# Mixing product ahead of phi of q in the queue of small work of 23 attention steps, and the second halves of the first two h scaled by Pool

## The chip, the cores and the metric

One core of a Trainium2 chip. The metric is the device time of one execution in microseconds (us). All runs but two are in the fast state, with a granted TensorE clock of 1.0: one run of the kernel before took 736.96 us and is left out of every comparison, and the single look of pool_probe (clock 0.996) is of unknown state and is compared with nothing. "TensorE" is the matrix engine (PE, with PEld for its weight loads), "VectorE" is DVE, "ScalarE" is ACT, "Pool" is GpSimd.

## The reference

It adds three things: the input x, a causal linear-memory attention over its layer norm, and a token-mixing MLP over the layer norm of that norm. Sizes: 2048 tokens, 1024 channels, 32 heads of 32, four segments of 512 tokens, 3584 hidden units.

```python
def _A_ref(x, wq, wk, wv, wo, beta):
    # q, k, v = x @ wq, x @ wk, x @ wv, as (B, H, N=4 segments, L=512, Dh=32)
    phi = lambda t: jnp.where(t > 0, t + 1.0, jnp.exp(t))
    for s in range(N):
        p = _softmax(jnp.einsum('bhqd,bhkd->bhqk', qs, ks) * scale + mask)
        a_dot = jnp.einsum('bhqk,bhkd->bhqd', p, vs)
        pq = phi(qs)
        a_mem = jnp.einsum('bhld,bhde->bhle', pq, M) / (jnp.einsum('bhld,bhd->bhl', pq, z)[..., None] + 1e-06)
        outs.append(g * a_mem + (1.0 - g) * a_dot)
        M, z = M + (phi(ks) against vs), z + (sum of phi(ks))
    return o @ wo

def _B_ref(x, w1, b1, w2, b2):
    h = _layernorm(x)
    u = _gelu(jnp.einsum('bsd,sf->bdf', h, w1) + b1)
    return transpose(jnp.einsum('bdf,fs->bds', u, w2) + b2)

x = A_x; xn = _layernorm(x)
return x + _A_ref(xn, ...) + _B_ref(xn, ...)
```

## The kernel before

The MLP runs first (until about 385 us), then the attention, in 32 steps: step u computes unit u (one segment, four heads) and finishes unit u-1. In the traces VectorE's operations of a step stand in the order in which they are issued (step 15 before: mtmp 515.49, pqT 515.81, prod 516.42). Semaphores are set from the lists `reads` and `writes`.

**The head.** The first rows are normalised while TensorE already waits for them. In the order string, `S` is the reciprocal root (a small addition on VectorE, then a power on Pool), `h` the scaling of a row, and a `'` marks its second half of 512 columns:

```python
NORM_ORDER = (["D0 A1 A1' A3 S0 h0 h0' S1 d2 h1 d2' S2 h1' h2 d4 A3' A5 S3 d4' h3"] + ...)

def rstd(self, c):                                   # "S"
    fw.op("dve", ... var = var * a + E_H)            # L609
    fw.op("pool", ... rs = pow(var, expo))           # L611

def scale_h(self, c, parts):                         # "h", "h'"; rows 0 and 1 in two halves
    for h0, h1 in parts:
        self.fw.op("dve", lambda e: e.tensor_scalar(both[:, h0:h1, c // 2, :], src, self.ln_mv[:, c, 0:1],
                                                    self.ln_rs[:, c, 1:2], op0=ALU.subtract, op1=ALU.mult), ...)  # L627
```

**The attention.** VectorE makes phi of q in two operations (`mtmp`, `pqT`), and the mixing of a unit's two outputs in four (`srec` twice, the mixing product `prod`, the sum `o_s`). Pool masks the exponentials of ScalarE. One group of matmuls, `weigh`, reads `pqT`:

```python
def phi(self, dst, R_dst, src, R_src, k, u):
    fw.op("dve", ... tensor_scalar(mt, et, 1.0, None, op0=ALU.min))                              # L1241, mtmp
    fw.op("dve", ... scalar_tensor_tensor(dst, src, 1.0, mt, op0=ALU.add, op1=ALU.max))          # L1243, pqT

def logits(self, u, step): ...
    fw.op("act", ... pT = exp(scores))                                                           # L1377
    for v, kb, _ in blocks:
        fw.op("pool", lambda e: e.affine_select(d, d, ...))                                      # L1381, the mask

def weigh(self, u, part): ...
    reads += [self.R_pqT[k], self.R_MZbf[g]]      # beside pT and vA: the group starts when all are there

def combine(self, u): ...
    return [scales, products, add]                # srec (L1474, L1475), prod (L1478), o_s (L1484)

def wo_job(self, c, half): ...
    def end(b): fw.op("dve", ... fin = bank + fin)          # L1320: also hands the bank back to TensorE

# the step u
    self.dense(cuts[0]); self.logits(u, 0); self.dense(cuts[1], end)
    self.weigh(u - 1, 0) ... self.weigh(u - 1, 2)            # with pieces of dense work between
    steps = self.combine(u - 1)
    self.side.append(steps.pop(0))                           # srec
    if N_GRP <= u:
        self.side.append(lambda u=u: self.phi_q(u))          # mtmp, pqT
    self.side.extend(steps)                                  # prod, o_s
    self.side.append(lambda u=u: (self.phi_k(u + 1), self.k_transpose(u + 1)))
    ...                                                      # dense, logits(u, 1); even steps also logits(u, 2)
```

`self.side` is a queue of small work that is issued, piece by piece, between the matmuls. `pqT` of unit u is thus made in step u and read by `weigh(u, 0)` in step u+1.

## Time and profile before

| | before |
|---|---|
| median (fast runs) | 652.8 us |
| span of the profiled run | 651.1 us |
| TensorE busy | 645.8 us |
| VectorE, ScalarE, Pool busy | 428.1, 281.4, 153.9 us |

Busy time says that TensorE is full, but not how full (the prediction says why). What matters is a hole between two starts. A line of a timeline reads: start, length (us), engine, source line, operation, output<-inputs, shape, how many instructions in a row; in brackets the idle time of the engine before it and what ended that. The lines themselves are in the prediction.

### The profile page before, as it was taken

Reading aid. Unit: us, or ns where it says so; the run is one execution under the profiler, and the core shown is the slowest. Engines: PE = TensorE matmul, PEld = TensorE weight load, DVE = VectorE, ACT = ScalarE, POOL = GpSimd, SP = SyncE. Lnnn points to the kernel's source line nnn. Section 1 sums busy time; section 2 is a strip of 40 time slices with the busy share of each in tenths; the row PEclk is TensorE's granted clock in tenths of the full one; section 3 lists DMA queues with packets and bytes.
Section 4 is the critical chain, followed back from the end, with each engine's and each line's share of the span. In section 5 each row is a group of like instructions: output and inputs, shape, how many; then the busy total and the mean of one; then the engine's idle time right before and its main releaser. Section 6 shows DMA issues by size and latency. Waiting matters only on the chain.

```text
span 651.1 us, 11170 instructions
## 1 busy us (share of the span) xinstructions
PE 645.8 (99%) x4611; PEld 303.2 (47%) x4611; DVE 428.1 (66%) x800; ACT 281.4 (43%) x305; POOL 153.9 (24%) x179
## 2 busy tenths in 40 slices
PE   8999999999999999999999999999999999999998
PEld 3444444444444444444444444444544444445544
DVE  6975675665556664744738325766787877777896
ACT  7543232232210000110101047778767778888770
POOL 2500000000011220220202203343334444554440
DMA  9804233242498967538262946988544456445325
GB/s 306 212 0 130 65 106 89 64 116 79 129 257 206 270 205 209 156 103 229 80 208 98 267 126 174 179 169 197 120 116 96 125 147 109 126 98 128 106 93 139
DMA packets 181963, 95.00 MB, mean 146 GB/s; under 512 B 100248, under 2 KB 167832, under 8 KB 181656
## 3 DMA queue, kind: packets, MB, share of 16 engines
q1 hardware_dynamic: 181768, 94.25, 56.3%
q8 instruction: 36, 0.59, 0.4%
q14 instruction: 15, 0.12, 0.1%
q10 hardware_dynamic: 144, 0.03, 0.0%
HBM read 69.23 MB, written 13.63 MB: 127 GB/s over the span
## 4 chain that ended last, share of the span: by engine, by line
PE 91%; DVE 5%; ACT 2%; DMA 2%; issue 1%; POOL 0%; DVEq 0%
PE ps_all L199 91%; ACT pT L1377 1%; DMA w2s<-in_B_w_dram 1%; DVE prod L1478 1%; DVE ln_st L587 1%; DVE sum L648 0%; DMA xin<-in_A_x_dram 0%; DVE mtmp L1243 0%; DVE h L627 0%; DVE mtmp L1241 0%; DVE fin L1320 0%; DVE ost L1431 0%; DVE kT L1275 0%; POOL ln_rs L611 0%; DVE part L689 0%
## 5 line engine op out<-in xcount | busy, mean ns | idle before, releaser
L1377 ACT ACTIVATE pT<-ps_all 128x2048 bf16<-128x2048 f32 x80 | 150.2, 1877 | 47.7 <-PE ps_all L199 47.2
L1381 POOL TENSOR_SCALAR_AFFINE_SELECT pT<-pT 128x512 bf16<-128x512 bf16 x128 | 105.3, 841 | 161.3 <-ACT pT L1377 161.3
L689 DVE TENSOR_TENSOR part<-ps_all,part 128x512 f32<-128x512 f32 x84 | 57.7, 690 | 109.1 <-PE ps_all L199 88.2
L1080 POOL TENSOR_TENSOR part<-part,stg 128x512 f32<-128x512 f32 x24 | 33.0, 1403 | 285.5 <-DVE part L689 285.5
L746 ACT ACTIVATE g<-part,b1c 128x512 f16<-128x512 f32 x36 | 26.0, 722 | 99.1 <-DVE part L689 99.1
L199 PE MATMUL ps_all<-wv,xnT 128*128 128x512 bf16 x256 | 68.6, 380 | 0.2
L199 PE MATMUL ps_all<-xnT,wq 128*128 128x512 bf16 (+1 forms) x256 | 66.4, 380 | 0.0
L199 PE MATMUL ps_all<-wo,oT 128*128 128x512 bf16 (+2 forms) x272 | 63.8, 367 | 0.1
L1431 DVE TENSOR_TENSOR ost<-ps_all,eps 128x396 bf16<-128x396 f32 (+1 forms) x72 | 37.1, 522 | 33.9 <-PE ps_all L199 33.3
L694 ACT ACTIVATE part<-ps_all 128x512 f32<-128x512 f32 x24 | 14.0, 596 | 101.6 <-PE ps_all L199 67.1
L199 PEld LDWEIGHTS ps_all<-vA,pT 128*128 128x128 bf16 x1280 | 45.7, 96 | 20.4 <-DVE ost L1431 1.7
L199 PE MATMUL ps_all<-g,w2s 128*128 128x512 f16 x224 | 51.0, 379 | 0.0
L199 PE MATMUL ps_all<-g,sum 128*128 128x512 f16 x224 | 51.0, 379 | 0.0
L199 PE MATMUL ps_all<-gT,sum 128*128 128x512 f16 x224 | 50.3, 379 | 0.2 <-DVE gT L663 0.2
L199 PE MATMUL ps_all<-vA,pT 128*128 128x33 bf16 x1280 | 48.5, 177 | 0.3 <-DVE ost L1431 0.3
L199 PE MATMUL ps_all<-h,sum 128*128 128x512 f16 x192 | 45.2, 379 | 0.0
L199 PE MATMUL ps_all<-h,w1s 128*128 128x512 f16 x192 | 44.9, 379 | 0.0
L199 PE MATMUL ps_all<-hT,sum 128*128 128x512 f16 x192 | 43.6, 379 | 0.0
L199 PEld LDWEIGHTS ps_all<-wo,oT 128*128 128x128 bf16 x272 | 23.8, 98 | 24.7 <-issue 3.7
L199 PEld LDWEIGHTS ps_all<-xnT,wq 128*128 128x128 bf16 x256 | 22.6, 97 | 25.4 <-issue 5.3
L199 PEld LDWEIGHTS ps_all<-gT,sum 128*128 128x128 f16 x224 | 21.8, 98 | 26.8 <-DVE gT L663 0.6
L199 PEld LDWEIGHTS ps_all<-g,w2s 128*128 128x128 bf16 x224 | 21.9, 98 | 26.4
(118 smaller groups left out, 867.7 us busy)
## 6 DMA issues: line engine op xcount, KB each, us to landing
w2s<-in_B_w_dram SPq DMA_DIRECT2D x8, 1792.0 KB, 9.7
w1s<-in_B_w_dram SPq DMA_DIRECT2D x12, 1024.0 KB, 5.6
wq<-in_A_wq_dram SPq DMA_DIRECT2D x32, 256.0 KB, 3.2
stg<-in_A_x_dram SPq DMA_DIRECT2D x16, 256.0 KB, 2.9
xs<-in_A_x_dram SPq DMA_DIRECT2D x16, 256.0 KB, 3.3
out_dram<-stg SPq DMA_DIRECT2D x16, 256.0 KB, 3.7
wk<-in_A_wk_dram SPq DMA_DIRECT2D x16, 256.0 KB, 3.6
fin<-out_dram SPq DMA_DIRECT2D x16, 256.0 KB, 3.3
```

The lines of the kernel that those rows point to most:

```text
L199: ins = self.nc.tensor.matmul(*args, **kwargs)
L587: fw.op("dve", lambda e: e.bn_stats(st[:, 6 * h:6 * h + 6], src[:, 512 * h:512 * h + 512]), reads=[self.R_xin[c]], writes=[R])
L689: self.fw.op("dve", lambda e: e.tensor_tensor(self.tmp[dst][:], self.bank(b), self.tmp[src][:], op=ALU.add), reads=[self.R_bank[b], self.R ...
L694: self.fw.op("act", lambda e: e.activation(self.tmp[dst][:], self.bank(b), ACT.Copy), reads=[self.R_bank[b]], writes=[self.R_tmp[dst]])
L746: self.fw.op("act", lambda e: e.activation(self.gB[f % 2][half][:, f // 2, :], src, ACT.Gelu_apprx_tanh, bias=self.b1c[:, f:f + 1], scale= ...
L1080: fw.op("pool", lambda e: e.tensor_tensor(self.tmp[t][:], self.tmp[t][:], self.stg[k][:, 512 * half:512 * half + 512], op=ALU.add), reads= ...
L1377: fw.op("act", lambda e: e.activation(dst, src, ACT.Exp, scale=SCALE), reads=self.R_bank[0:4], writes=[R[v % 2][kb] for v, kb, _ in blocks ...
L1381: fw.op("pool", lambda e: e.affine_select(d, d, pattern=[[0, 4], [1, P]], compare_op=ALU.is_ge, fill=0.0, base=0, channel_multiplier=-1), ...
L1431: fw.op("dve", lambda e: e.tensor_tensor(dst, src, eps, op=ALU.add), reads=[self.R_bank[b], self.R_eps], writes=[self.R_ost[o][part]])
L1478: fw.op("dve", lambda e: e.tensor_tensor(self.prod[:], ost[:, :, 0:D_HEAD], rec.unsqueeze(2).to_broadcast([P, 32, D_HEAD]), op=ALU.mult), ...
```

## The change

The intent: in the attention, the long product of VectorE goes first, so that it doesn't keep Pool's masks waiting; in the head, two half rows are given to an idle engine.

```diff
-    NORM_ORDER = (["D0 A1 A1' A3 S0 h0 h0' S1 d2 h1 d2' S2 h1' h2 d4 A3' A5 S3 d4' h3"] +
+    NORM_ORDER = (["D0 A1 A1' A3 S0 h0 h0' S1 d2 h1 h1' d2' S2 h2 d4 A3' A5 S3 d4' h3"] +
@@ scale_h
-            self.fw.op("dve", lambda e: e.tensor_scalar(both[:, h0:h1, c // 2, :], src, self.ln_mv[:, c, 0:1],
+            self.fw.op("pool" if h0 else "dve", lambda e: e.tensor_scalar(both[:, h0:h1, c // 2, :], src, self.ln_mv[:, c, 0:1],
@@ the step
                 self.side.append(steps.pop(0))
+            if u > N_GRP:
+                self.side.append(steps.pop(0))
             if N_GRP <= u:
                 self.side.append(lambda u=u: self.phi_q(u))
```

## The prediction

> **What bounds the kernel now.** I read the page first, then the waits of the TensorE weight loads, then the timeline of every engine around each gap found there, then the head.
>
> ```profile
> PE 645.8 (99%) x4611; PEld 303.2 (47%) x4611; DVE 428.1 (66%) x800; ACT 281.4 (43%) x305; POOL 153.9 (24%) x179
> PE ps_all L199 91%; ACT pT L1377 1%; DMA w2s<-in_B_w_dram 1%; DVE prod L1478 1%; DVE ln_st L587 1%; DVE sum L648 0%; DMA xin<-in_A_x_dram 0%; DVE mtmp L1243 0%; DVE h L627 0%; DVE mtmp L1241 0%; DVE fin L1320 0%; DVE ost L1431 0%; DVE kT L1
> ```
>
> TensorE bounds it from end to end: 91% of the chain of work is its matmuls. Its 99% hides small holes, because a matmul is shown as 0.38 us long while the next one starts 0.216 us after it (four in a row take 1.03 us: three starts and one length). So I looked for holes between the starts. In the whole middle (25 to 375 us) there is one of 0.3 us, at 183 us, which waits for a weight transfer that this change does not touch. What VectorE and Pool can be blamed for is small: three holes in the head, together 0.67 us, and six in the attention, together about 1.3 us (0.31 at 473.6, 0.32 at 484, 0.32 at 503, 0.08 at 519, 0.15 each at 548 and 578). The other attention holes end with ScalarE, so I leave them. That is 2.0 us of 651: no outcome of these edits can approach the 13 us that 2% would be, unless something new breaks.
>
> The head, in the timeline (start, length, engine, line, operation):
>
> ```profile
> 6.23 0.73 DVE L627 TENSOR_SCALAR h<-xin,ln_mv,ln_rs 128x512 f16<-128x512 bf16 x2 [0.75 <-POOL ln_rs L611]
> 6.76 2.29 PEld L199 LDWEIGHTS ps_all<-h,w1early 128*128 128x128 bf16 x12 [0.93 <-DMA w1early<-in_B_w_dram]
> 9.13 0.40 DVE L627 TENSOR_SCALAR h<-xin,ln_mv,ln_rs 128x512 f16<-128x512 bf16 x1
> 9.29 0.65 POOL L611 TENSOR_TENSOR ln_rs<-ln_mv,expo 128x1 f32<-128x1 f32 x1 [1.64 <-DVE ln_mv L609]
> 9.59 0.55 PEld L199 LDWEIGHTS ps_all<-h,w1early 128*128 128x128 bf16 x4 [0.55 <-DVE h L627]
> 10.05 0.55 DVE L627 TENSOR_SCALAR h<-xin,ln_mv,ln_rs 128x1024 f16<-128x1024 bf16 x1 [0.51 <-POOL ln_rs L611]
> 10.71 1.42 PEld L199 LDWEIGHTS ps_all<-h,w1early 128*128 128x128 bf16 x8 [0.57 <-issue]
> 12.64 22.13 PEld L199 LDWEIGHTS ps_all<-h,w1early 128*128 128x128 bf16 x104 [0.50 <-DVE ln_mv L609]
> ```
>
> TensorE waits at 9.59 for the second half of h1, at 10.71 for h2, at 12.64 for h3; after that 104 loads go without a hole. What sets 12.64 is the row of statistics on VectorE and the small powers on Pool (0.55 us each), not the half of h1: that half (9.13) lies in the shadow of Pool's power (9.29 to 9.94), and VectorE still idles 0.51 us before h2.
>
> The attention: a masking pair of Pool beside the phi and mixing work of VectorE, in three steps.
>
> ```profile
> 468.54 1.22 POOL L1381 TENSOR_SCALAR_AFFINE_SELECT pT<-pT 128x512 bf16<-128x512 bf16 x2 [3.46 <-ACT pT L1377]
> 469.14 0.77 DVE L1241 TENSOR_SCALAR mtmp<-etmp 128x512 bf16<-128x512 bf16 x1
> 474.12 0.11 PEld L199 LDWEIGHTS ps_all<-wo,oT 128*128 128x128 bf16 x2 [0.42 <-DVE kT L1275]
> ...
> 479.82 2.32 POOL L1381 TENSOR_SCALAR_AFFINE_SELECT pT<-pT 128x512 bf16<-128x512 bf16 x2 [3.52 <-ACT pT L1377]
> 480.00 1.65 DVE L1478 TENSOR_TENSOR prod<-ost,srec 128x1024 bf16<-128x1024 bf16 x1
> 481.68 0.74 DVE L1484 TENSOR_TENSOR o_s<-prod 128x512 bf16<-128x512 bf16 x1
> 484.48 0.21 PEld L199 LDWEIGHTS ps_all<-vA,pT 128*128 128x128 bf16 x6 [0.65 <-DVE ost L1431]
> ...
> 546.50 1.22 DVE L1478 TENSOR_TENSOR prod<-ost,srec 128x1024 bf16<-128x1024 bf16 x1
> 546.71 1.50 POOL L1381 TENSOR_SCALAR_AFFINE_SELECT pT<-pT 128x512 bf16<-128x512 bf16 x1 [2.78 <-ACT pT L1377]
> 548.33 0.18 PEld L199 LDWEIGHTS ps_all<-vA,pT 128*128 128x128 bf16 x4 [0.45 <-issue]
> ```
>
> Alone, a mask takes 0.63 us, prod 1.22, o_s 0.42, the short phi operation (mtmp) 0.29, pqT 0.69. Side by side they stretch: the mask at 546.71 takes 1.50 us and ends 0.49 us after prod does (548.21 against 547.72), and the next weight load of TensorE is at 548.33. I take that one, called "issue" by the view, for a wait on this mask. At 480.00 it is prod that is stretched, by 0.43 us, after the mask had started 0.18 us ahead of it.
>
> [...] prod 1.22 or 1.65 us, mask 0.63 or 1.50. [...] a VectorE operation behind a mask loses 0.31 to 0.48 us, less than the mask's 0.63. [...] No Pool tensor_scalar is in this trace; the mask, with one input of the same 512 columns, took 0.63 us, which I use as the estimate.
>
> **The change, part by part.** No matmul, transfer or ScalarE instruction is added or moved in order; the instruction lists show only VectorE and Pool rows changed.
>
> *Head.* Two VectorE scalings of 0.40 us go; two Pool ones appear, each behind the power of its own row. Gain to be had: TensorE's hole at 9.59 (0.22 us) closes, but TensorE then waits longer for h2 at 10.71, so this alone is worth nothing. VectorE's first h0 half no longer precedes a second one, so the variance of row 1 is scaled at most 0.06 us earlier, and Pool's power at 9.29, now without h1' beside it, takes 0.55 instead of 0.65: together at best -0.15 us on h2 and h3. Loss to be had: Pool can start h0' about 0.05 us after its power ends at 6.11, VectorE starts h0 at 6.23. [...] h0 loses about 0.35 us. That only eats slack at 6.76 (TensorE has 0.49 us of holes before 10.71). Again at 7.66, Pool's h1' comes before VectorE's h1 (7.77): h1 ends about 0.38 late, the statistics of row 2 behind it as well, the power too, less the 0.10 won: h2 and h3 about +0.28 us. With a slow Pool scaling of 1.4 us (a Pool addition of 512 columns takes 1.40) it would be about +0.5. I weigh these to +0.2 us.
>
> *Attention, 23 steps from the tenth on.* VectorE's work is the same; prod moves about 0.9 us earlier, mtmp and pqT about 1.2 us later. In the step of 480: prod would run 479.07 to 480.29 without a stretch, the first mask [...] then goes, mtmp waits until about 480.63 and ends 480.92, pqT waits behind the second mask and ends near 481.96, o_s at 482.3 against 482.42: VectorE is 0.11 us ahead, and the hole at 484 shrinks by that. The steps of 503 and 519 have the same order: 0.11 and 0.08. At 469: mtmp saves 0.48, prod loses about 0.35: 0.13 us on the hole at 474. At 546 and 576: prod runs 545.57 to 546.79, mtmp to 546.99, the mask ends about 547.5 instead of 548.21, so both holes of 0.15 us close. Sum: 0.11 + 0.11 + 0.08 + 0.13 + 0.30 = 0.73 us; a tenth or so will be lost to other waits: -0.65 us. pqT comes later by 1.2 us, but its reader is in the next step: pqT at 552.80 ends 553.49, the weigh that needs it starts 556.48, so 3 us of slack become some 1.7.
>
> Sum of both parts: -0.65 + 0.2 = -0.45 us; 652.9 - 0.45 = 652.4.
>
> **Rivals.** (a) pqT becomes the wait: for it, it is delayed in each step and its two operations now meet the masks (up to 0.35 us each); against it, the slack of 1.7 us. The last step is tightest: pqT ends 633.52, its reader starts 635.70; moved behind prod and a mask it would end near 635. If it were late in many steps by 0.2 us: +2 to +4 us, 655 to 657. (b) [...] the stretch that prod loses, o_s and pqT take over, and VectorE ends up to 0.3 us later in the short steps, where selects start after prod today; then the holes at 474, 484 and 503 stay and only the two of 0.15 us close: 652.7 with the head. (c) The head costs more than the attention yields, because h0 and h1 collide with Pool: 653.0 to 653.2. (d) Nothing shows at all, as TensorE's next wait (ScalarE's exponentials, 0.43 us before many loads) ends where it did: 652.8.
>
> **Range and chances.** The largest total gain by my list is 0.15 + 0.85 = 1.0 us, the likely loss at most 0.5 us with nothing gained; repeat runs differ by 0.1 us. So 651.8 to 653.2 should hold 8 times in 10. Faster by 2% would need 13 us where 2 us of holes exist: 0.5%. Slower by 2% would need rival (a) at four times my worst: 1%. Within 2%: 98.5%.
>
> **What would show each step.** Head: two Pool scalings of 0.6 to 0.8 us after 6.15 and 7.7; the load now at 9.59 without a hole before it; the one at 12.64 at 12.5 to 13.0. If Pool's scaling took over 1.2 us, my head is too cheap. Attention: prod at 1.22 us nearly everywhere instead of up to 1.65, mtmp and pqT stretched instead; first masks of the short steps at 0.7 to 0.9 instead of 1.50 us; no hole at 548 and 578; those at 474, 484, 503 at 0.2. New waits of TensorE on pqT would prove me wrong, as would an unchanged mask ahead of 548.

What no trace or run shows is cut from it, where marked. -0.65 us for the attention and +0.2 for the head make -0.45, so 652.4. That h0 loses 0.35 us and h1 0.38 was meant for the case that Pool's scaling starts first; both are estimates, worked out from what operations of VectorE lose beside a mask in the trace, from 0.31 us (mtmp of k at 472.47, 1.00 against 0.69) to 0.48 (mtmp at 469.14, 0.77 against 0.29). So are the waits of mtmp and pqT behind a mask in the step of 480 (0.34 and 0.35 us): the trace shows longer times beside a mask, not a wait for one. The 0.05 us between Pool's power and its scaling was an estimate too (0.11 measured, from 6.11 to 6.22). Of repeat runs, which the text has 0.1 us apart, the four fast ones of the kernel before lie within 0.31 us.

## The result, and the profile after

| | before | after |
|---|---|---|
| median of 5 runs | 652.82 us | 658.95 us |
| range of the fast runs | 652.59 to 652.9 (one slow run of 736.96 left out) | 658.8 to 659.76 |
| ratio of fast runs | | 1.0097, 95% interval 1.0082 to 1.0112 |
| span of the profiled run | 651.1 | 657.1 |

A ratio here is the mean time of one kernel's fast runs over that of the other's of the same rounds, so not quite the ratio of the medians. The change costs 6 us: within 2%, as predicted, but far outside the range of 651.8 to 653.2. The page of the kernel after (busy times, then the shares of the chain of work):

```profile
PE 646.8 (98%) x4611; PEld 303.0 (46%) x4611; DVE 435.2 (66%) x798; ACT 281.6 (43%) x305; POOL 143.1 (22%) x181
PE 89%; DVE 7%; ACT 2%; POOL 1%; issue 1%; DMA 0%; DVEq 0%
```

Busy times hint at what happened, but not at its size: Pool has two scalings more and is still 10.8 us less busy; VectorE has two instructions less and is 7.1 us more busy. Of the waits of the weight loads, summed by what ended them (us in total, times, longest), these differ. Before:

```profile
PEld ps_all L199 <- DVE fin L1320: 0.8, 2, 0.4
PEld ps_all L199 <- DVE pqT L1243: 0.5, 2, 0.2
```

After:

```profile
PEld ps_all L199 <- DVE pqT L1243: 5.3, 7, 1.3
PEld ps_all L199 <- DVE fin L1320: 2.5, 2, 1.2
PEld ps_all L199 <- POOL h L627: 2.3, 2, 1.2
```

These are the three culprits. The idle time of a weight load overstates what TensorE loses: before, the loads of the weigh of step 15 start at 517.22, 0.21 us ahead of its first matmul (517.43), and after, the 1.34 us of idle time before its loads are only 1.01 us between the matmuls. So I set the start of each matmul of one trace against the same one of the other and noted where the distance jumps:

| at (us, before) | TensorE then waits for | jump (us) |
|---|---|---|
| 7.7 to 12.6 | h0' and h1' of Pool, and the rows behind | +1.85 |
| 183 | a weight transfer (8.3 us before, 8.0 after) | -0.31 |
| 474, 519 | holes of the kernel before that shrink | -0.12, -0.08 |
| 508.8, 524.5 | fin, which frees a bank | +0.87, +0.87 |
| 463, 517, 533, 548, 563, 578 | pqT | +0.29, +1.01, +0.58, +0.29, +0.29, +0.29 |
| 614.7 | | +0.08 |

The sum is 5.9 of the 6.0 us: 1.85 in the head, 2.75 by pqT, 1.74 by fin, the rest small.

**The head after.** Pool's timeline, and below it the loads of TensorE:

```profile
6.22 2.21 POOL L627 TENSOR_SCALAR h<-xin,ln_mv,ln_rs 128x512 f16<-128x512 bf16 x1
8.40 0.56 POOL L611 TENSOR_TENSOR ln_rs<-ln_mv,expo 128x1 f32<-128x1 f32 x1
9.07 2.20 POOL L627 TENSOR_SCALAR h<-xin,ln_mv,ln_rs 128x512 f16<-128x512 bf16 x1
11.24 0.56 POOL L611 TENSOR_TENSOR ln_rs<-ln_mv,expo 128x1 f32<-128x1 f32 x1
```

```profile
8.48 0.55 PEld L199 LDWEIGHTS ps_all<-h,w1early 128*128 128x128 bf16 x4 [1.16 <-POOL h L627]
11.32 0.55 PEld L199 LDWEIGHTS ps_all<-h,w1early 128*128 128x128 bf16 x4 [1.16 <-POOL h L627]
14.49 0.55 PEld L199 LDWEIGHTS ps_all<-h,w1early 128*128 128x128 bf16 x4 [0.50 <-DVE ln_mv L609]
```

A half row takes Pool 2.2 us, against 0.40 on VectorE. The reader should see the second line of Pool: the power of row 1, which stood at 7.11 before, now runs at 8.40, directly behind the scaling. TensorE's first load of h3 moves from 12.64 to 14.49.

**An odd step (15).** VectorE and TensorE before:

```profile
515.49 0.28 DVE L1241 TENSOR_SCALAR mtmp<-etmp 128x512 bf16<-128x512 bf16 x1
515.81 0.69 DVE L1243 SCALAR_TENSOR_TENSOR pqT<-qT,mtmp 128x512 bf16<-128x512 bf16 x1
516.42 1.65 DVE L1478 TENSOR_TENSOR prod<-ost,srec 128x1024 bf16<-128x1024 bf16 x1
...
517.22 0.36 PEld L199 LDWEIGHTS ps_all<-vA,pT 128*128 128x128 bf16 x4
```

After:

```profile
518.08 1.21 DVE L1478 TENSOR_TENSOR prod<-ost,srec 128x1024 bf16<-128x1024 bf16 x1
519.21 0.72 DVE L1241 TENSOR_SCALAR mtmp<-etmp 128x512 bf16<-128x512 bf16 x1
519.97 1.00 DVE L1243 SCALAR_TENSOR_TENSOR pqT<-qT,mtmp 128x512 bf16<-128x512 bf16 x1
...
521.02 0.17 PEld L199 LDWEIGHTS ps_all<-vA,pT 128*128 128x128 bf16 x4 [1.34 <-DVE pqT L1243]
```

Before, pqT ended at 516.50 and the weigh that reads it began its loads at 517.22, so 0.72 us of slack. After, the weigh starts as soon as pqT ends (520.97). Counted from the end of srec (514.97 and 517.56), pqT ends after 1.53 and after 3.41 us: 1.88 late, which is 1.16 more than the slack, and 1.01 of it shows between the matmuls. In step 19 the delay is 2.02 us (0.92 and 2.94 after srec) and the slack was 1.75 (pqT ended 546.58, the loads began 548.33): 0.29 shows.

The delay of 2.0 us of step 19 is the 1.22 of prod, 0.44 more on mtmp, 0.31 more on pqT, and a few hundredths for the pause that prod now has behind srec. The first was the intent; the other two are what I call the stretch: beside Pool's masks mtmp takes 0.72 us in place of 0.28 and pqT 1.00 in place of 0.69, and without the masks (nomask_swap, below) both means are back at 286 and 692 ns. What the two engines contend for, no trace here shows. VectorE's group lines for the attention (times summed, mean ns of one, idle before) and Pool's masks, before:

```profile
L1243 DVE SCALAR_TENSOR_TENSOR pqT<-qT,mtmp 128x512 bf16<-128x512 bf16 x24 | 16.6, 692 | 0.8
L1381 POOL TENSOR_SCALAR_AFFINE_SELECT pT<-pT 128x512 bf16<-128x512 bf16 x128 | 105.3, 841 | 161.3 <-ACT pT L1377 161.3
```

After:

```profile
L1243 DVE SCALAR_TENSOR_TENSOR pqT<-qT,mtmp 128x512 bf16<-128x512 bf16 x24 | 23.8, 992 | 0.8
L1381 POOL TENSOR_SCALAR_AFFINE_SELECT pT<-pT 128x512 bf16<-128x512 bf16 x128 | 90.2, 722 | 180.0 <-ACT pT L1377 180.0
```

A pqT is now stretched by 0.30 us in the mean; the mean of mtmp goes from 309 to 476 ns; prod falls from 1316 to 1239, o_s from 709 to 544, a mask from 841 to 722. The masks did win what the change meant them to win. Nobody was waiting for most of it.

**An even step (14).** VectorE's fin, Pool's masks and TensorE behind them, before:

```profile
506.94 2.31 POOL L1381 TENSOR_SCALAR_AFFINE_SELECT pT<-pT 128x512 bf16<-128x512 bf16 x2 [3.34 <-ACT pT L1377]
506.95 1.22 DVE L1478 TENSOR_TENSOR prod<-ost,srec 128x1024 bf16<-128x1024 bf16 x1
508.08 0.68 DVE L1320 TENSOR_TENSOR fin<-ps_all,fin 128x512 bf16<-128x512 f32 x1
...
508.82 0.76 PEld L199 LDWEIGHTS ps_all<-wv,xnT 128*128 128x128 f16 x5 [0.38 <-DVE fin L1320]
```

After:

```profile
507.85 1.22 DVE L1478 TENSOR_TENSOR prod<-ost,srec 128x1024 bf16<-128x1024 bf16 x1
508.65 1.55 POOL L1381 TENSOR_SCALAR_AFFINE_SELECT pT<-pT 128x512 bf16<-128x512 bf16 x2 [3.33 <-ACT pT L1377]
509.00 0.72 DVE L1241 TENSOR_SCALAR mtmp<-etmp 128x512 bf16<-128x512 bf16 x1
509.75 1.00 DVE L1243 SCALAR_TENSOR_TENSOR pqT<-qT,mtmp 128x512 bf16<-128x512 bf16 x1
510.68 0.68 DVE L1320 TENSOR_TENSOR fin<-ps_all,fin 128x512 bf16<-128x512 f32 x1
...
511.41 0.76 PEld L199 LDWEIGHTS ps_all<-wv,xnT 128*128 128x128 f16 x5 [1.25 <-DVE fin L1320]
```

In both orders fin stands behind the same three operations (mtmp, pqT, prod). Before, they took 1.98 us from the end of srec (506.10 to 508.08); after, 2.87 (507.81 to 510.68). The difference of 0.89 us is the jump of 0.87. Here the order itself costs little (0.12 to 0.13 us is left once the masks are taken away, below): nearly all of it is the stretch. A pair of masks comes up while prod runs. In the old order prod is the last of the three: the pair takes 2.31 us and runs on beside fin, which is not stretched by it (0.68 us, and 0.68 in the kernel after, where the pair is over at 510.20). In the new order mtmp and pqT still follow, and each of them is stretched beside a mask (0.72 us in place of 0.29, 1.00 in place of 0.69).

### The profile page after: what moved, and what is told of

It reads as the page before. It is cut to its first block, busy times and chain, and to the rows that moved or that the text cites. A ratio compares the mean times of both kernels' runs of the same rounds, so it can differ in the third digit from the quotient of the medians.

```text
span 657.1 us, 11150 instructions
## 1 busy us (share of the span) xinstructions
PE 646.8 (98%) x4611; PEld 303.0 (46%) x4611; DVE 435.2 (66%) x798; ACT 281.6 (43%) x305; POOL 143.1 (22%) x181
## 4 chain that ended last, share of the span: by engine, by line
PE 89%; DVE 7%; ACT 2%; POOL 1%; issue 1%; DMA 0%; DVEq 0%
PE ps_all L199 89%; DVE prod L1478 1%; ACT pT L1377 1%; DVE pqT L1243 1%; DVE mtmp L1241 1%; DVE ost L1431 1%; POOL h L627 1%; DVE fin L1320 1%; DMA xin<-in_A_x_dram 0%; DVE ln_st L587 0%; DVE MZbf L1444 0%; DVE srec L1474 0%; DVE MZ L1442 0%; POOL ln_rs L611 0%; DVE srec L1475 0%
## 5 line engine op out<-in xcount | busy, mean ns | idle before, releaser
L1381 POOL TENSOR_SCALAR_AFFINE_SELECT pT<-pT 128x512 bf16<-128x512 bf16 x128 | 90.2, 722 | 180.0 <-ACT pT L1377 180.0
L199 PEld LDWEIGHTS ps_all<-g,sum 128*128 128x128 f16 x224 | 21.9, 98 | 26.4
```

Source lines behind the costliest of these rows:

```text
L199: ins = self.nc.tensor.matmul(*args, **kwargs)
L1381: fw.op("pool", lambda e: e.affine_select(d, d, pattern=[[0, 4], [1, P]], compare_op=ALU.is_ge, fill=0.0, base=0, channel_multiplier=-1), ...
```

## The experiments

All twelve were correct by the comparison and timed in several rounds against the kernel before, except one that was a single look. None of those timed differs from the kernel before by 2%; what follows rests on the smaller differences and on the traces. The kernel before had medians of 653.1, 652.6 and 652.7 us in the three groups. My theory after the result: (1) Pool's slow scaling, with the powers queued behind it, makes the head; (2) pqT late by prod plus the stretch makes the waits of the odd steps; (3) fin late, by the stretch and hardly by the order, makes those of two even steps. Rivals: the head and the attention push each other; the reorder alone, without the stretch, is the cost; a wait named pqT hides another.

### The two halves of the change

The head alone (edit: the order string and the engine, no reorder):

> The two half scalings on Pool, the attention as before. If Pool's 2.2 us a scaling holds back the powers behind it: TensorE 1.85 us late at 13 us, and 654.3 to 654.7 us in all, the lower number if the weight transfer at 170 us is again 0.3 us shorter. Rival: 652.9, if the head's delay is taken back in a later wait.

Measured: 654.5 us median, ratio 1.0023 (1.0008 to 1.0038). TensorE's jumps are the same +0.84, +0.27, +0.62, +0.12 as in the full change.

The attention alone:

```diff
+            if u > N_GRP:
+                self.side.append(steps.pop(0))
```

> The swap of mixing product and phi of q in the 23 steps, the head as before. By the jumps between the two traces (TensorE start against TensorE start) the attention lost 4.4 us and the head 1.5 us net. If the parts add: 657.2 us (656.9 to 657.5). Rival: the head's 1.5 us shifts the attention against its transfers and part of the 4.4 is that; then 656.5 or less.

Measured: 657.28 us, ratio 1.0066 (1.0051 to 1.0081). The two ratios add up to 1.0089, the full change has 1.0097; the intervals overlap. The traces say the same more closely: the jumps of each part come at the same places and sum to about the same as in the full change (1.85 and some 4.3 us). No sign is seen of the rival that the parts push each other.

### Odd and even steps

```diff
-            if u > N_GRP:
+            if u > N_GRP and u % 2 == 0:      # even_only; for odd_only: u % 2 == 1
                 self.side.append(steps.pop(0))
```

> The swap in even steps alone. Theory A (the late phi of q holds up the product that reads it, early in the next step) sees no hole here, as after an even step the reader comes 3 us later: 652.7 us. Theory B ([...] the whole row of VectorE ends later) sees the two holes of 0.87 us that end with a late fin addition: 652.8 + 1.74 - 0.15 = 654.4 us.

Theory B, here and below: VectorE's row is stretched beside the masks and ends later.

> The swap in odd steps alone, where the reader of pqT follows about 0.9 to 1.8 us behind it. Both theories: the six holes in front of the product that reads pqT, 0.29 + 1.01 + 0.58 + 3 x 0.29 = 2.75 us: 655.6 us (655.2 to 656.0). If even and odd do not add to the full swap (4.4 us), a step's delay is carried into the next one.

Measured: even 654.51 us, ratio 1.0023 (1.0009 to 1.0038); odd 655.97 us, ratio 1.0044 (1.0027 to 1.006). By their jumps, the even one has the two waits on fin (+0.87, +0.86) and the 0.12 us won at 474, and its waits on pqT are those of before (0.5 us in two); the odd one has the six waits on pqT (0.28, 1.01, 0.58, three of 0.29) and waits on fin as before. Sum of the excess: 0.67%, the attention alone 0.66%. So pqT is a matter of the odd steps, fin of the even ones. The odd one has a further +0.61 us in the tail, on a transfer of o_s, which the full change does not have; I take that for no part of the cause, without having tested it.

### Taking away the reader's wait

The weigh group is made to read the pqT of the unit before, which was done long ago. The result is wrong (the comparison with the reference doesn't notice it):

```diff
-        i, k, hl = (u // 4) % 3, u % 3, 4 * (g % 4)
+        i, k, hl = (u // 4) % 3, (u - (u > N_GRP)) % 3, 4 * (g % 4)
```

> The swap of all 23 steps, but from the second memory unit on the product reads the phi of q of the unit before (wrong on purpose), which has long been there; instructions and masks are the same. Theory A: the six holes in front of that product go, 2.75 of 4.4 us: 654.4 us. If instead the mask or the ost buffers hold that product up, nothing goes: 657.2. Theory B's fin holes (1.74 us) stay in either case.

Measured, with the reorder in: 653.93 us, ratio 1.0024 (1.0007 to 1.0041). Against the 1.0066 of the attention alone that is 0.42%, or 2.7 us less, where the jumps on pqT had summed to 2.75. No wait on pqT is left; the wait on fin stays:

```profile
PEld ps_all L199 <- DVE fin L1320: 2.5, 2, 1.2
```

The waits called pqT were thus real waits on pqT and hid nothing of size behind them. By the trace a little more comes free than expected: with pqT out of the way, the holes of 0.15, 0.08 and 0.15 us that the kernel before had at 548, 563 and 578 are closed. With the 0.12 at 474 and 0.08 at 519 that is 0.59 us won by the new order, of the 0.73 of the prediction's list.

### Taking away the masks

To take the stretch away, Pool's masks are left out, once in the old order and once in the new (wrong; the comparison again doesn't notice):

```diff
-            fw.op("pool", lambda e: e.affine_select(d, d, pattern=[[0, 4], [1, P]], compare_op=ALU.is_ge,
-                                                    fill=0.0, base=0, channel_multiplier=-1),
-                  reads=[self.R_pu[v % 2][kb]], writes=[self.R_pd[v % 2][kb]])
+            del d
```

> Kernel before with Pool's masks left out (wrong result on purpose: later tokens are seen). It is the base of the next run. If the two holes of 0.15 us at 548 and 578 us are waits for a mask that prod holds up, they go, and the VectorE row is 0.4 us a step shorter: 651.8 us (651.2 to 652.6). If they have another cause they stay.

> The swap of all 23 steps with the masks left out (wrong on purpose). Theory B [...] pqT comes 1.25 us later and no more; only steps with less than that to spare show holes (two of about 0.3 us): within 0.6 us of the run without masks and without swap. Theory A alone (prod's length in front of pqT is enough): most of the loss stays, 3 us or more over that run.

Measured: old order 651.87 us, ratio 0.9987 (0.9972 to 1.0002); new order 652.66, ratio 0.9999 (0.9984 to 1.0014). In the attention the new order now costs 0.52 us against the old (jumps of +0.12 at 508, +0.27 at 516, +0.13 at 523), where it cost 4.3 with the masks; another +0.41 comes at 639, where TensorE waits for a transfer in the tail. (By the medians the two orders lie 0.79 us apart, a little over the 0.6 expected; that transfer is the excess.) And pqT takes its undisturbed time again:

```profile
L1243 DVE SCALAR_TENSOR_TENSOR pqT<-qT,mtmp 128x512 bf16<-128x512 bf16 x24 | 16.6, 692 | 0.8
```

This tells the reorder from the stretch. The prod ahead (1.22 us) alone fits into the slack of every step but 15; the 0.75 us of the stretch on top of it don't. At 517 us the jump falls from 1.01 to 0.27 without masks, by 0.74, about the 0.75 of the stretch. The old order without masks also shows the most that a cure of the stretch could win here. By the times it is 0.13% (the interval goes from 0.28% faster to 0.02% slower). By the trace it is some 1.4 us: the holes at 548, 563 and 578 close (-0.15, -0.08, -0.15), as expected of waits on the mask, that at 519 too (-0.08), and so do those at 474, 484 and 503 (-0.30, -0.32, -0.32), so VectorE is late there because the masks stretch its row. (Some of this is TensorE's wait for the masks themselves, so 1.4 is a ceiling.) That is the size of the prize for which the change risked 4.3.

### What Pool's scaling costs by itself

Nine operations of Pool on dead tiles in the tail, after everything else (one look). Cut:

```diff
+        probes = [lambda e: e.tensor_scalar(o16, src, s0, s1, **two),             # L1660, as in the change
+                  ...
+                  lambda e: e.tensor_scalar(o16[:, 0:256], src[:, 0:256], s0, s1, **two),
+                  lambda e: e.tensor_scalar(o16, src, s0, None, op0=ALU.subtract),
+                  ...
+                  lambda e: e.tensor_copy(o16, src), ...]
```

> Kernel before with nine Pool operations on dead tiles behind the last masks, one after the other: the scaling as in the change twice, 256 columns of it, bf16 output, one operation, constants in place of columns, float32, and two copies. If the 2.2 us is Pool's own speed, the first two take 2.2 us [...], and 256 columns 1.1 to 1.3 us. [...] If the column operands make it slow, constants take half or less; if the 16-bit conversion does, float32 or bf16 output do.

Pool's timeline in the tail:

```profile
641.19 2.08 POOL L1660 TENSOR_SCALAR mtmp<-o_s,ln_mv,ln_rs 128x512 f16<-128x512 bf16 x1 [5.79 <-DVE o_s L1484]
...
645.54 1.22 POOL L1662 TENSOR_SCALAR mtmp<-o_s,ln_mv,ln_rs 128x256 f16<-128x256 bf16 x1
...
649.03 1.56 POOL L1664 TENSOR_SCALAR mtmp<-o_s,ln_mv 128x512 f16<-128x512 bf16 x1
...
654.85 0.61 POOL L1667 CAST mtmp<-o_s 128x512 f16<-128x512 bf16 x1
```

Here it takes 2.08 us, behind the last o_s, where VectorE of the kernel before is idle for 2.42 us; so the 2.2 of the head is nearly all Pool's own speed and hardly a stretch beside VectorE. 512 against 256 columns gives (2.08 - 1.22) / 256 = 3.4 ns for a column and 0.36 us for the instruction, an estimate from two lengths. Constants in place of the two columns (1.93), bf16 out (2.07) and float32 on both sides (2.07) change little; one operation in place of two takes 1.56; a plain cast or copy takes 0.61. Of what was varied, the two arithmetic operations cost most, though why is not shown: the mask's 0.63 us, on which I had rested my estimate, is the time of a copy.

### The two scalings one by one

```diff
-            self.fw.op("dve", lambda e: e.tensor_scalar(...
+            self.fw.op("pool" if h0 and c == 0 else "dve", ...     # head_h0; head_h1: c == 1, and the new order string
```

> Kernel before with one edit: only the second half of the first h (row 0) is scaled by Pool; everything else and the order of issue as before. My theory (Pool takes 2.2 us for a scaling of 512 columns, and the power of the next row is queued behind it on Pool): the scaling runs from about 6.2 to 8.4, the power of row 1 from 8.4 to 9.0 instead of about 7.1 to 7.7, so both halves of the second h come about 1.2 us later, TensorE waits for h0' by 0.8 to 0.9 us and everything behind is 1.1 to 1.4 us later: 653.9 to 654.2. Rival (only the TensorE's own wait for the half counts, the powers have slack): 653.5.

> Kernel before with one edit: only the second half of the second h (row 1) is scaled by Pool, issued where the changed kernel issues it. My theory: the scaling runs from about 7.7 to 9.9, the power of row 2 waits behind it and comes about 0.5 us later, TensorE waits for h1' until about 10.0 (0.4 us more than before) and for h2 0.5 us more than before: 653.1 to 653.5. With the run above this should add up to about the 1.85 us of the head of the changed kernel. Rival (the two halves cost the same, half of 1.85 each): 653.6.

Measured: h0' on Pool 653.76 us, ratio 1.0016 (1.0002 to 1.0029); h1' on Pool 653.01, ratio 1.0004 (0.9988 to 1.0019). The first two rows of Pool in the first of them:

```profile
6.04 2.21 POOL L627 TENSOR_SCALAR h<-xin,ln_mv,ln_rs 128x512 f16<-128x512 bf16 x1
8.23 0.56 POOL L611 TENSOR_TENSOR ln_rs<-ln_mv,expo 128x1 f32<-128x1 f32 x1
```

TensorE's first load of h3 comes at 13.76 there and at 13.18 with h1', against 12.64 before: 1.12 and 0.54 later, together 1.66 of the 1.85 us of the full head. (In the first of these runs the whole norm started 0.18 us earlier, 6.05 against 6.23 for the first scaling, which is most of the gap; both also have 0.31 us less at 183.) Both medians lie some 0.1 us below the ranges, less than the transfer at 183 took off. By the times h1' on Pool can't be told from no change; it is the traces that separate the two. By them the first half costs twice the second. TensorE's own wait for h0' is a jump of 0.84, but h3 doesn't wait for it: in head_h0 the power of row 1 comes 1.12 us later (8.23 against 7.11), and so does the load of h3 (1.12). That speaks for the powers queued on Pool, and the statistics of the later rows behind them; no run takes the powers away from Pool, so this step rests on the traces.

### Other cures for the same holes

If the order is left alone, VectorE can be given less to do where TensorE waits for it. The holes at 474, 484 and 503 end with kT or ost on VectorE; they are the three that also closed without the masks. ScalarE can copy kT out of its bank as well:

```diff
+            if u in (12, 13, 15):
+                fw.op("act", lambda e: e.activation(self.kT[k][:], self.bank(b), ACT.Copy),
+                      reads=[self.R_bank[b]], writes=[self.R_kT[k]])
+            else:
                 fw.op("dve", lambda e: e.tensor_copy(self.kT[k][:], self.bank(b)), ...)
```

> Kernel before with another edit: the three copies of kT in steps 12, 13 and 15 are made by ScalarE instead of VectorE, so that VectorE reaches the prod, o_s and ost rows ahead of TensorE's holes at 474, 484 and 503 some 0.4 us earlier. My theory (the holes that the change aimed at belong to VectorE's queue in these steps): holes of 0.31, 0.32 and 0.32 us go or shrink to below 0.1: 651.9 to 652.2 against 652.7. Rival (ScalarE has no room there: its exponentials come as much later as the copy takes): 652.6 to 653.2, with new waits of TensorE on pT.

Measured: 651.68 us, ratio 0.9985 (0.9972 to 0.9997). The jumps are -0.295, -0.319 and -0.322 at exactly the three holes, -0.94 together; the rest of the trace's gain (0.3 us at 183, 0.1 in the head) isn't the edit's. The load that stood at 474.12 behind a wait of 0.42 us on kT now has none:

```profile
473.20 0.32 PEld L199 LDWEIGHTS ps_all<-wo,oT 128*128 128x128 bf16 x2
```

The second edit adds a prod in two halves where Pool's mask is what TensorE waits for:

```diff
+            for a, z in ((0, 16), (16, 32)) if u in (18, 22) else ((0, 32),):
+                fw.op("dve", ... prod[:, a:z, :] = ost[:, a:z, :] * rec[:, a:z] ...)
```

> As k_by_act, and prod in two halves in the steps of units 18 and 22, [...]. My theory: the two holes of 0.15 us at 548 and 578 go as well: 0.2 to 0.3 us faster than k_by_act, 651.6 to 651.9. Rival ([...] pqT and fin come later [...]): the same as k_by_act or slower.

Measured: 651.5 us, ratio 0.9983 (0.9971 to 0.9996). The mask at 546.71 of the kernel before took 1.50 us; here it takes 0.98 and ends (546.61) before the second half of prod does (547.15), where it ended 0.49 us after the whole one. The two halves together take 1.72 us, the whole took 1.22. The holes at 548 and 578 close (-0.15 each), and about 0.07 us of each comes back 2 us later. By the times, the two versions can't be told apart (651.26 to 652.56 against 651.49 to 651.98); by the trace the split is worth some 0.15 us, less than the 0.2 to 0.3 expected. This is the best version: 0.17% below the kernel before.

## Why the prediction was right or wrong

- **What bounds the kernel, and how much can be won: right.** TensorE from end to end, with about 2 us of holes that VectorE and Pool could be blamed for. The kernel without masks won 0.13%, and the best version 0.17%.
- **"Within 2%": right**, at +0.97%, but the reason given (2 us of holes) bounds only a gain. The text's "unless something new breaks" is what happened, at a cost of 6 us; the most that it had set aside for that was the 4 us of rival (a). **The range: wrong**, since it allowed for a loss of 0.5 us at the most and each of the two parts lost more than that.
- **Head, the term of Pool's scaling: wrong in size.** The step "the mask, with one input of the same 512 columns, took 0.63 us, which I use as the estimate" failed: it took 2.2. Even the bad case, 1.4 from a Pool addition, was too cheap. At 0.63 us the power of row 1 would have found Pool free by 6.9, before its turn at 7.1, so the queue behind the scaling was not in my sum; at 2.2 it is most of it. The term was +0.2 us and measured +1.85. The text did say that over 1.2 us would make it too cheap. The wait that its +0.28 was built on, h1 stretched beside Pool's scaling, did not come: h0 and h1 took 0.41 us on VectorE beside Pool's scalings.
- **Attention, the masks: right in the short steps.** First masks 0.70 us where they took 1.50 (step 19), prod at 1.22, the hole at 474 smaller by 0.12, that of 519 gone. (For the steps of 546 and 576 the sum let mtmp pass ahead of the mask unstretched; measured, the mask passed first and mtmp took 0.72. And the 0.85 us that the range allows the attention to win is not the 0.73 of its own list.)
- **Attention, "3 us of slack become some 1.7": wrong, and the main failure.** It was read in an even step (552.80, step 20), where the reader comes late: 2.8 to 5.9 us of slack in even steps, 0.72 to 2.23 in odd ones, 0.72 to 1.75 in the six that now wait. "The last step is tightest" was misread too: it has 2.18, step 15 has 0.72. And the delay is not 1.2 but 2.0: the stretch of mtmp and pqT beside the masks stood in rival (a), as "up to 0.35 us each", and was left out of the sum. Measured: 0.44 and 0.31. Rival (a), with 655 to 657, is the one that came about (odd_only alone took 655.97, but by six waits of 0.29 to 1.01 us and not by 0.2 in many steps); odd_only, oldpq_swap and nomask_swap show it.
- **Attention, fin: not foreseen by any rival.** Rival (b), by which the stretch passes from prod to other operations, came nearest (pqT went from 692 to 992 ns in the mean), but looked at o_s and the selects and not at the operation that frees a bank. It costs 1.74 us, and even_only shows it alone. What rival (b) says of the holes also held: those at 484 and 503 stayed.
- **The holes at 548 and 578: half right.** I took the first for a wait on the mask; splitting prod there, which lets the mask go earlier, closes it. In the changed kernel that wait is gone too (the mask ends at 552.38, the weigh starts at 553.62), but pqT takes its place; oldpq_swap, without the wait on pqT, has both holes closed.
- **484 and 503 smaller by 0.1: wrong**; they kept their size. They belong to VectorE's queue, which the change did not shorten, since it only moved the masks' stretch from one operation to another; they close when a copy is taken from that queue (k_by_act) or the stretch is (nomask_plain).

## What to carry to other kernels

Before something is put ahead of a producer, measure the slack to its reader in every kind of step, not in one that is easy to read, and add to the delay what the moved order does to operations that run beside those of another engine: here the stretch went from Pool's masks (841 to 722 ns), which had time, to the pqT that TensorE reads (692 to 992 ns). Before a small operation goes to an idle engine, measure that very operation on it, and look at what is queued behind it there: here a 0.40 us scaling became 2.2 us in front of the powers that every later row needs. When the holes are known one by one, the cheap cure is to take work from the queue that ends them (three copies to another engine, -0.94 us), not to rearrange the queue of every step.
